# Attention, Fourier mixing and two MLPs on one core: the matmul that sums a pair's squares moves behind the step's score product in batches 2 and 3

## The chip, the cores and the metric

One core of a Trainium2 chip runs the whole program in one launch. The metric is device time in microseconds (us). The kernel before took 1077.4 us, the median of three runs (1074.99 to 1078.43).

## What is computed

Four batches of 8 heads, 576 tokens, head width 64. Cut to what matters:

```python
scores = q @ k.T / sqrt(64); bias = min(-(cum_i - cum_j), 0)   # cum = cumsum(relu(s))
attn = softmax(where(causal, -1e9, scores + bias)) @ v
x = attn.reshape(B, S, 512)
u = x + real(fft(fft(x, axis=1), axis=2))
x2 = u + relu(layernorm(u) @ w1) @ w2                # first MLP, 512 -> 2048 -> 512
out = x2 + relu((layernorm(x2) * g) @ w1b) @ w2b     # second MLP, same widths
```

## The kernel before, in words

**Order of the work.** The main stream is `MlpStream.run` (L582): the first MLP of a batch, chunk by chunk (L451 and L475 are its two products). Between two of its steps `side()` lets a generator emit work of the batches that come next: attention of batch b+1, then that batch's Fourier mixing (`fft_steps`), then its layer norm. So attention of batch 2 is woven into the MLP of batch 1, and attention of batch 3 into the MLP of batch 2; for batch 2 the first six pieces come earlier still, beside the mixing of batch 1. The second MLP runs last, alone (L517, L545).

The order in which each engine finally gets its instructions is not the order of the source text. A scheduler (L1572) places them on a modelled timeline by priority; an earlier place in the program is a higher priority, `urgent` (L1312) raises it for attention by a given number of places, and `tc.issue_after(x)` adds that an instruction on the engine of `x` must stand behind `x` there. Each engine works its queue off in that order.

**Attention in batches 2 and 3.** `attn_steps` (L933) goes over the batch's 4 pairs of heads. A pair has ten units (five tiles of queries, A0, A1, M, B0, B1, by two heads), one per step `j` = 0 to 9. In a step, `emit_qk` (L811) writes each unit's scores: per tile and head two fp16 products (L821, L822) into one PSUM tile, in two halves for B0. DVE then adds the bias and takes the minimum (L823), ACT makes two exponentials (L856, L857), POOL or DVE the low half (L867), SP a transposing DMA (L871, L879), and seven steps later `emit_pv` (L883) multiplies by v (L899). In these batches A0 has two units in steps 0 and 1, and B0 follows in steps 2 and 3 (in pairs 8 and 12, the first of their batches, A1).

**Preparation of the next pair.** The steps also prepare pair p (8 to 11 in batch 2, 12 to 15 in batch 3) while pair p-1 is worked on; pair 8 alone is prepared ahead of its batch. `prep_pair` (L722) is a generator, advanced once a step from `j` = 1 on:

- `j` = 1: three ACT squares of q, k and v with a sum along the free axis (L728) into `mx`, then `total(mx)` (L88): one fp32 matmul of `mx` with a matrix of ones (L92) that sums over the partitions. The trace has two records for each such matmul.
- `j` = 2: `pow2_scale` (L101 to L106 on DVE) and two products of scales (L735, L738).
- `j` = 3: high and low half of q (L746 on ACT, L747 on DVE).
- `j` = 4: the same of k (L753, L757), then one transposing DMA of q and k (L762) on SP.
- `j` = 5: v (L1069, L1070).

`load_pair` (L696, loads L691 to L709 on SP) fills `raw` for the pair after. When pair p begins, `turn_pair` (L773 on DVE) reverses a part of what the transposing DMA wrote, and the first score reads it.

`total` and the scores take their PSUM tiles from the same pool, `ps_s`, of three (L43); the tile of `total` is free again when L101 has read it. In batches 0 and 1 another path (`prep_pair32`, `emit_qk32`) does the same with fp32 products and sums the squares of v alone.

```python
        mxa = total(mx)
        yield
        sc = scs[:, p % 8, :]
        pow2_scale(sc[:, 0:3], sc[:, 3:6], mxa, 15)
```

Of the kernel before, what the change touches and what calls it, by code (L numbers as in the profile page):

```python
# [33 lines left out]
def fused_kernel(ctx: ExitStack, tc, q, k, v, s, wa1, wa2, g_ln, wb1, wb2, tok_c, feat_c, ident_c, rev_c, bias_c, out):  # L34
    nc = tc.nc
# [19 lines left out]
    def ftile(name, t, h):  # L55
        return ring.tile([128, FW[t]], F32, tag=f"f{t}{h}", name=name)
# [31 lines left out]
    def total(parts):  # L88

        n = parts.shape[1]  # L90
        ps = ps_s.tile([128, 512], F32, tag="s", name="total")[:, 0:n]
        nc.tensor.matmul(out=ps, lhsT=ones.to_broadcast([128, 128]), rhs=parts, start=True, stop=True)  # L92
        return ps

    def pow2_scale(dst, inv, squares, limit):

        top = int((127 + limit + 63.5 - 0.05) * 2 ** 23)
        d = dst.bitcast(I32)  # L100
        nc.vector.tensor_scalar(  # L101
            out=d, in0=squares.bitcast(I32), scalar1=-0.5, scalar2=float(top), op0=ALU.mult, op1=ALU.add
        )
        nc.vector.tensor_scalar(out=d, in0=d, scalar1=float(167 << 23), scalar2=float(67 << 23), op0=ALU.min, op1=ALU.max)
        nc.vector.tensor_scalar(out=d, in0=d, scalar1=0x7F800000, scalar2=None, op0=ALU.bitwise_and)
        nc.vector.tensor_scalar(  # L106
            out=inv.bitcast(I32), in0=d, scalar1=-1.0, scalar2=float(254 << 23), op0=ALU.mult, op1=ALU.add
        )
# [609 lines left out]
    def scale_cum(p, h):  # L718
        P = pairs[p]
        nc.scalar.activation(out=P.cumb[h], in_=P.cumb[h], func=AF.Copy, scale=P.sc[:, 6:7])  # L720

    def prep_pair(p):  # L722

        P = pairs[p]
        b, hp = divmod(p, NPAIR)
        mx = small.tile([128, 3], F32, tag="mx", name="mx")
        for i in range(3):
            nc.scalar.activation(  # L728
                out=qk16[:, i].rearrange("p t n -> p (t n)").bitcast(BF16), in_=raw[:, i].rearrange("p t h d -> p (t h d)"), func=AF.Square, accum_out=mx[:, i:i + 1]
            )  # L730
        mxa = total(mx)
        yield
        sc = scs[:, p % 8, :]
        pow2_scale(sc[:, 0:3], sc[:, 3:6], mxa, 15)
        nc.vector.tensor_scalar(  # L735
            out=sc[:, 6:7], in0=sc[:, 0:1], scalar1=sc[:, 1:2], scalar2=8.0, op0=ALU.mult, op1=ALU.mult
        )
        nc.vector.tensor_scalar(  # L738
            out=sc[:, 7:8], in0=sc[:, 3:4], scalar1=sc[:, 4:5], scalar2=-0.125, op0=ALU.mult, op1=ALU.mult
        )  # L740
        P.sc = sc
        yield

        for h in range(2):
            hi = qk16[:, h, :, 64 * h:64 * h + 64]
            nc.scalar.activation(out=hi, in_=raw[:, 0, :, h, :], func=AF.Copy, scale=sc[:, 0:1])  # L746
            nc.vector.scalar_tensor_tensor(  # L747
                out=qk16[:, h, :, 64 - 64 * h:128 - 64 * h], in0=raw[:, 0, :, h, :], scalar=sc[:, 0:1], in1=hi,
                op0=ALU.mult, op1=ALU.subtract,
            )  # L750
        yield
        for h in range(2):
            nc.scalar.activation(  # L753
                out=qk16[:, 2 + h].rearrange("p t (r d) -> p t r d", r=2),
                in_=raw[:, 1, :, h:h + 1, :].to_broadcast([128, 5, 2, D]), func=AF.Copy, scale=sc[:, 1:2],
            )
            nc.vector.scalar_tensor_tensor(  # L757
                out=qk16[:, 4 + h, :, 64 * h:64 * h + 64], in0=raw[:, 1, :, h, :], scalar=sc[:, 1:2],
                in1=qk16[:, 2 + h, :, 0:64], op0=ALU.mult, op1=ALU.subtract,
            )  # L760
        P.qkT = qkTs[p % 2]
        nc.sync.dma_start_transpose(  # L762
            out=P.qkT.rearrange("p b (t n) -> p (b t) n", n=128), in_=qk16.rearrange("p b t n -> p (b t n)")
        )
        yield
        P.v = v_tile()
        split_v(P, raw[:, 2].rearrange("p t h d -> p t (h d)"))
# [7 lines left out]
    def q_rows(P, t, h):  # L775
        if t in (B0, B1):
            return P.qx[:, h, QX[t]]
        return P.qkT[:, h, QCOLS[t]]
# [32 lines left out]
    def emit_qk(us):  # L811

        P, t = pairs[us[0].p], us[0].t
        n = EXT[t]
        cuts = ((0, 288), (288, 576)) if n > 512 else ((0, n),)
        mns = [small.tile([128, 2], F32, tag="mn", name="mn", bufs=4) for _ in us]
        kT, qTs = P.qkT, [q_rows(P, t, u.h) for u in us]
        for i, (a, z) in enumerate(cuts):
            for u, mn, qT in zip(us, mns, qTs):
                ps = ps_s.tile([128, 512], F32, tag="s", name="s")[:, 0:z - a]  # L820
                nc.tensor.matmul(out=ps, lhsT=qT, rhs=kT[:, 2 + u.h, a:z], start=True, stop=False)  # L821
                nc.tensor.matmul(out=ps, lhsT=qT, rhs=kT[:, 4 + u.h, a:z], start=False, stop=True)  # L822
                gate[0] = nc.vector.tensor_tensor_reduce(  # L823
                    out=u.f[:, a:z], in0=ps, in1=u.f[:, a:z], scale=P.sc[:, 7:8],
                    scalar=mn[:, i - 1:i] if i else 3.0e38, op0=ALU.add, op1=ALU.min, accum_out=mn[:, i:i + 1],
                )
        for u, mn in zip(us, mns):
            emit_exp(u, mn[:, len(cuts) - 1:len(cuts)])
# [10 lines left out]
    def emit_exp(u, mn):  # L839
        P, t, h = pairs[u.p], u.t, u.h  # L840
        n = EXT[t]
        if h == 0 and u.k % 2 == 0:
            sums[0] = small.tile([128, 4], F32, tag="rs", name="rs", bufs=4)
        u.both = sums[0]
        u.rs = sums[0][:, 2 * (u.k % 2):2 * (u.k % 2) + 2]
        w = NKB[t] * 128
        if t in (B0, B1):
            u.w = htile("p16", t, h, 0)
            if w > n:
                nc.gpsimd.memset(u.w[:, 0:2 * w].rearrange("p (r w) -> p r w", r=2)[:, :, n:w], 0.0)  # L850
        elif h == 0:
            P.w[t] = htile2("p16", t, 0)
            u.w = P.w[t][:, 0:2 * w]
        else:
            u.w = P.w[t][:, 2 * w:4 * w]
        nc.scalar.activation(out=u.w[:, 0:n], in_=u.f[:, 0:n], func=AF.Exp, bias=mn, scale=-1.0)  # L856
        nc.scalar.activation(  # L857
            out=u.f[:, 0:n], in_=u.f[:, 0:n], func=AF.Exp, bias=mn, scale=-1.0, accum_out=u.rs[:, h:h + 1]
        )
# [205 lines left out]
    def v_tile():  # L1065
        return att.tile([128, 5, 2, 128], F16, tag="v16", name="v16", bufs=2)

    def split_v(P, rv):
        nc.scalar.activation(out=P.v[:, :, 0, :], in_=rv, func=AF.Copy, scale=P.sc[:, 2:3])  # L1069
        nc.vector.scalar_tensor_tensor(  # L1070
            out=P.v[:, :, 1, :], in0=rv, scalar=P.sc[:, 2:3], in1=P.v[:, :, 0, :], op0=ALU.mult, op1=ALU.subtract
        )

    def emit_qk32(u):
        P, t, h = pairs[u.p], u.t, u.h
        n = EXT[t]
        pe = u.p < NPAIR
        block = {A0: 1, A1: 129, M: 0, B1: 320, B0: 448}[t]
        if pe:
            u.f = ftile("sc", t, h)  # L1080
            g = 2 * u.p + h
        cuts = ((0, 288), (288, 576)) if n > 512 else ((0, n),)
        mn = small.tile([128, 2], F32, tag="mn", name="mn", bufs=4)
        for i, (a, z) in enumerate(cuts):
            ps = ps_s.tile([128, 512], F32, tag="s", name="s")[:, 0:z - a]
            if pe:
                nc.tensor.matmul(
                    out=ps, lhsT=PB["sel"][:, g:g + 1].to_broadcast([96, 128]), rhs=PB["k"][:, a:z], start=True, stop=False
                )
            masked = pe and a <= block < z  # L1090
            nc.tensor.matmul(  # L1091
                out=ps, lhsT=P.qT[:, QCOLS[t]], rhs=P.kT[h][:, a:z], start=not pe, stop=not masked,
            )
            if masked:
                nc.tensor.matmul(out=ps[:, block - a:], lhsT=PB["eye"], rhs=PB[t], start=False, stop=True)
            gate[0] = nc.vector.tensor_tensor_reduce(  # L1096
                out=u.f[:, a:z], in0=ps, in1=PB["zero"].to_broadcast([128, z - a]) if pe else u.f[:, a:z], scale=-1.0,
                scalar=mn[:, i - 1:i] if i else 3.0e38, op0=ALU.add, op1=ALU.min, accum_out=mn[:, i:i + 1],
            )
        emit_exp(u, mn[:, len(cuts) - 1:len(cuts)])  # L1100
# [475 lines left out]
```

## Time and profile before

| | us |
|---|---|
| median of three runs | 1077.4 |
| the profiled execution | 1072.82 |
| its span, first to last instruction | 1071.0 |
| PE busy in it | 964.8 (90%) |
| DVE busy | 670.8 (63%) |
| ACT busy | 588.3 (55%) |
| POOL busy | 458.7 (43%) |
| mean granted TensorE clock, share of full speed | 0.968 |

PE is TensorE's matmul, PEld its weight load, DVE VectorE, ACT ScalarE, POOL GpSimd, SPq the queue on SyncE that issues DMAs. A row of a timeline gives start in us, length in us, engine, line, operation, output and inputs by the program's names, and in brackets how long the engine was idle just before and what ended that. Several like instructions in a row are merged (x18). The sums of q, k and v are 3 columns wide (128x3), which tells the eight matmuls at issue from the others on L92.

### The profile page before, as it was taken

How to read it: one execution, taken by the hardware profiler on the slowest of the kernel's cores; microseconds unless marked ns; L12 is line 12 of the kernel's file. 1: busy time of each engine (PE TensorE's matmuls, PEld its weight loads, DVE VectorE, ACT ScalarE, POOL GpSimd, SP SyncE). 2: the span in 40 equal slices, each digit the busy share in tenths (PEclk: the TensorE clock that was granted, in tenths of full speed). 3: DMA queues.
4: the chain of work that ended last, by engine and by line, in shares of the span. 5: the costliest groups of instructions: out<-in, count | busy, mean ns of one | idle time of the engine just before them, and what ended most of it. 6: DMA issues, size and time to landing. Idle time of an engine off the chain costs nothing.

```text
span 1071.0 us, 22888 instructions
## 1 busy us (share of the span) xinstructions
PE 964.8 (90%) x8665; PEld 738.3 (69%) x8665; DVE 670.8 (63%) x1659; ACT 588.3 (55%) x1263; POOL 458.7 (43%) x766
## 2 busy tenths in 40 slices
PE   4676659998989899979989989899999999999998
PEld 3444337666666576657766656678888888888887
DVE  5989889657794464956559969754543543542342
ACT  5788659775695653777533466444444434343341
POOL 3535344544373551545610042454543544543452
PEclk9889878999999999999999999999999999999999
DMA  6999966986599980699934852021121111111000
GB/s 199 273 183 276 228 171 128 165 154 115 126 164 192 186 155 1 125 203 168 206 96 136 287 177 60 21 59 21 41 51 31 40 39 43 40 40 21 21 21 21
DMA packets 289063, 125.47 MB, mean 117 GB/s; under 512 B 272696, under 2 KB 272952, under 8 KB 286904
## 3 DMA queue, kind: packets, MB, share of 16 engines
q1 hardware_dynamic: 288312, 121.90, 51.4%
q0 software_dynamic: 640, 2.10, 0.7%
q8 instruction: 68, 1.11, 0.4%
q14 instruction: 43, 0.35, 0.1%
HBM read 61.50 MB, written 9.51 MB: 66 GB/s over the span
## 4 chain that ended last, share of the span: by engine, by line
PE 52%; DVE 20%; DMA 9%; issue 8%; ACT 5%; POOL 3%; SPq 3%; DVEq 0%; POOLq 0%; ACTq 0%
PE acc L545 15%; PE g1x L517 9%; PE g L517 9%; PE g L451 7%; PE g L475 6%; PE pv L899 2%; POOL p L867 2%; DMA pT<-p 2%; PE s L1091 2%; DMA wastage<-in_moe_w_ch_dram 2%; DMA first<-first 1%; DVE h L458 1%; DVE wblow L192 1%; DVE sc L823 1%; DMA unT<-u 1%
## 5 line engine op out<-in xcount | busy, mean ns | idle before, releaser
L451 PE MATMUL g<-unT,warows 128*128 128x256 f16 (+1 forms) x1920 | 220.4, 265 | 4.5 <-DMA unT<-u 3.8
L451 PEld LDWEIGHTS <-warows 128*128 128x128 f16 x1920 | 174.9, 99 | 44.8 <-issue 7.9
L475 PE MATMUL g<-wastage,h 128*128 128x512 f16 x756 | 184.4, 384 | 7.2 <-DVE h L458 5.1
L517 PEld LDWEIGHTS <-wbrows 128*128 128x128 f16 x1728 | 169.1, 98 | 20.2
L867 POOL TENSOR_TENSOR p<-sc,p 128x448 f16<-128x448 f32 (+4 forms) x152 | 142.1, 946 | 93.4 <-ACT sc L857 73.4
L531 DVE TENSOR_TENSOR wastage<-wastage 128x896 f16<-128x896 f32 x72 | 78.5, 1090 | 160.2 <-ACT wastage L530 157.7
L545 PEld LDWEIGHTS <-wastage 128*128 128x128 f16 x1512 | 147.9, 98 | 17.1
L475 PEld LDWEIGHTS <-h 128*128 128x128 f16 x864 | 82.9, 99 | 93.8 <-DVE h L458 11.6
L530 ACT CAST wastage<-wastage 128x896 f16<-128x896 f32 x72 | 67.5, 938 | 120.6 <-POOL wastage L528 120.6
L856 ACT ACTIVATE p<-sc,mn 128x576 f16<-128x576 f32 (+4 forms) x160 | 89.6, 576 | 43.5 <-DVE mn L823 17.1
L527 POOL TENSOR_TENSOR wastage<-wastage 128x128 f32<-128x128 f32 x72 | 51.4, 714 | 133.5 <-ACT wastage L524 133.5
L899 PEld LDWEIGHTS <-pT 128*128 128x128 f16 x1632 | 63.0, 100 | 56.5 <-DMA pT<-p 42.5
L899 PE MATMUL pv<-v,pT 128*128 128x64 f16 x1632 | 68.9, 196 | 36.5 <-DMA pT<-p 28.0
L517 PE MATMUL g1x<-unT,wbrows 128*128 128x256 f16 x864 | 101.5, 273 | 0.0
L517 PE MATMUL g<-unT,wbrows 128*128 128x256 f16 x864 | 100.9, 273 | 0.0
L857 ACT ACTIVATE sc<-sc,mn 128x576 f32<-128x576 f32 (+4 forms) x160 | 91.7, 574 | 1.3
L545 PE MATMUL acc<-wbbig,wastage 128*128 128x256 f16 x756 | 89.9, 273 | 0.0
L545 PE MATMUL acc<-wblow,wastage 128*128 128x256 f16 x756 | 87.9, 273 | 0.0
L804 POOL TENSOR_SCALAR_AFFINE_SELECT sc<-cumb 128x129 f32<-128x129 f32 (+4 forms) x120 | 61.8, 527 | 47.7 <-ACT cumb L720 26.0
L1091 PE MATMUL s<-first 128*128 128x288 f32 (+4 forms) x192 | 72.6, 476 | 3.6 <-DVE mn L1096 2.1
L458 DVE SCALAR_TENSOR_TENSOR h<-g,h 128x512 f16<-128x512 f32 (+1 forms) x80 | 50.4, 629 | 28.1 <-ACT h L457 27.8
L850 POOL MEMSET p<- 128x128 f16 x64 | 13.5, 212 | 114.9 <-DMA pT<-p 76.6
(239 smaller groups left out, 1553.0 us busy)
## 6 DMA issues: line engine op xcount, KB each, us to landing
wbbig<-in_moe_w_ch_dram SPq DMA_DIRECT2D x8, 1024.0 KB
wbbig<-in_moe_w_ch_dram SPq DMA_DIRECT2D x16, 512.0 KB
cumb<-cumd SPq DMA_DIRECT2D x24, 288.0 KB
wastage<-in_moe_w_ch_dram SPq DMA_DIRECT2D x6, 1024.0 KB
xset<-in_moe_w_ch_dram SPq DMA_DIRECT2D x9, 512.0 KB
x2d<-o SPq DMA_DIRECT2D x18, 256.0 KB
first<-in_q_dram SPq DMA_DIRECT2D x64, 64.0 KB
first<-in_k_dram SPq DMA_DIRECT2D x32, 128.0 KB
```

Of the source, the lines that this page charges most:

```text
L451: nc.tensor.matmul(out=ps[:, c * i:c * i + c], lhsT=ch.w.w1(lw, kk, m + i), rhs=ch.unT[:, 4 * lx + kk, 0:c], start=(n == 0), stop=(n == 23),)
L475: nc.tensor.matmul(out=ch.ps[j], lhsT=h[:, lh, c:c + 128], rhs=ch.w.w2(lw, m + i), start=(m + i + n == 0), stop=(m + i == MB - 1 and n == 2),)
L517: nc.tensor.matmul(out=ps, lhsT=ch.w.w1(lw, kk, m + 8 * half), rhs=ch.unT[:, 4 * lx + kk, :], start=(n == 0), stop=(n == 11),)
L530: nc.scalar.copy(out=h[:, 0], in_=r[:, 0:7])
L531: nc.vector.tensor_tensor(out=h[:, 1], in0=r[:, 0:7], in1=h[:, 0], op=ALU.subtract)
L545: nc.tensor.matmul(out=acc[key], lhsT=h[:, lh, ia], rhs=b[:, ib, lw], start=(m == 0 and i == 0 and not second), stop=(m == 7 and i == 2 an ...
L804: nc.gpsimd.affine_select(out=u.f[:, 0:n], in_=P.cumb[u.h][:, 0:n], pattern=[[-1, n]], compare_op=ALU.is_ge, fill=MASKED, base=base, chann ...
L856: nc.scalar.activation(out=u.w[:, 0:n], in_=u.f[:, 0:n], func=AF.Exp, bias=mn, scale=-1.0)
L857: nc.scalar.activation(out=u.f[:, 0:n], in_=u.f[:, 0:n], func=AF.Exp, bias=mn, scale=-1.0, accum_out=u.rs[:, h:h + 1])
L867: eng.tensor_tensor(out=u.w[:, w:w + n], in0=u.f[:, 0:n], in1=u.w[:, 0:n], op=ALU.subtract)
L899: nc.tensor.matmul(out=ps[:, c], lhsT=pT[:, lp * nb + kb, :], rhs=P.v[:, kb, lv, c], start=(n == 0), stop=(n == 3 * nb - 1),)
L1091: nc.tensor.matmul(out=ps, lhsT=P.qT[:, QCOLS[t]], rhs=P.kT[h][:, a:z], start=not pe, stop=not masked,)
```

## The change

`total(mx)` is emitted in the step after the squares, ahead of `pow2_scale`, and it must stand on PE behind the last score product emitted so far. `last_qk` holds that product; the two functions that emit scores set it.

```diff
+    last_qk = [None]
+
     def prep_pair(p):
...
-        mxa = total(mx)
         yield
+        with tc.issue_after(last_qk[0].ins):
+            mxa = total(mx)
         sc = scs[:, p % 8, :]
         pow2_scale(sc[:, 0:3], sc[:, 3:6], mxa, 15)
...
                 nc.tensor.matmul(out=ps, lhsT=qT, rhs=kT[:, 2 + u.h, a:z], start=True, stop=False)
-                nc.tensor.matmul(out=ps, lhsT=qT, rhs=kT[:, 4 + u.h, a:z], start=False, stop=True)
+                last_qk[0] = nc.tensor.matmul(out=ps, lhsT=qT, rhs=kT[:, 4 + u.h, a:z], start=False, stop=True)
...
             if pe:
-                nc.tensor.matmul(
+                last_qk[0] = nc.tensor.matmul(
                     out=ps, lhsT=PB["sel"][:, g:g + 1].to_broadcast([96, 128]), rhs=PB["k"][:, a:z], start=True, stop=False
                 )
             masked = pe and a <= block < z
-            nc.tensor.matmul(
+            last_qk[0] = nc.tensor.matmul(
                 out=ps, lhsT=P.qT[:, QCOLS[t]], rhs=P.kT[h][:, a:z], start=not pe, stop=not masked,
             )
```

## Rows read from the trace of the kernel before

**Rows 1.** Busy time by stretch: PE, PEld, DVE, ACT, POOL, clock, DMA share, GB/s

```profile
270.00:400.00 130.00, 117.58 (x1140) 83.78 (x1139) 84.60 (x270) 88.95 (x212) 65.38 (x116) 0.97 0.87 165
...
430.00:540.00 110.00, 101.76 (x1101) 71.80 (x1100) 77.28 (x260) 75.60 (x180) 57.30 (x92) 0.97 0.94 188
```

**Rows 2.** Who waited for whom, 250 to 520 us: sum, times, longest

```profile
DVE scs L101 <- PE total L92: 11.5, 5, 5.0
...
PE s L821 <- DMA first<-first: 5.9, 3, 4.4
...
PE total L92 <- ACT first L728: 5.3, 2, 4.0
```

**Rows 3.** The instructions of L92: count, ns min/median/max, first and last start

```profile
L92 PE MATMUL total<-mx,ones x32: 167/252/373, 16.0 to 492.2; 128*128 128x1 f32 x16, 128*128 128x3 f32 x16
```

**Rows 4.** Timeline around the sum for pair 12

```profile
362.40 1.01 PE L899 MATMUL pv<-v,pT 128*128 128x64 f16 x29
...
366.49 0.74 ACT L728 ACTIVATE first<-first 128x640 bf16<-128x640 f32 x1 [4.41 <-DMA first<-in_v_dram]
...
367.38 0.38 PE L92 MATMUL total<-mx,ones 128*128 128x3 f32 x2 [3.96 <-ACT first L728]
367.51 0.18 PEld L821 LDWEIGHTS <-first 128*128 128x128 f16 x1
...
367.68 0.26 PE L822 MATMUL s<-first 128*128 128x129 f16 x1
...
368.26 3.54 PE L451 MATMUL g<-unT,warows 128*128 128x256 f16 x18
```

**Rows 5.** Busy time and granted clock by microsecond after that wait

```profile
367.00:368.00 1.00, 0.62 (x6) 0.56 (x7) 0.16 (x1) 0.32 (x2) 0.00 (x0) 0.86 1.01 182
368.00:369.00 1.00, 1.00 (x6) 0.70 (x5) 0.92 (x5) 0.49 (x2) 0.20 (x1) 0.50 1.15 214
...
371.00:372.00 1.00, 1.00 (x11) 0.85 (x9) 0.00 (x0) 1.00 (x3) 0.00 (x0) 0.93 1.07 276
```

**Rows 6.** Timeline around the sum for pair 14

```profile
461.84 0.38 PE L92 MATMUL total<-mx,ones 128*128 128x3 f32 x2 [1.36 <-ACT first L728]
...
462.44 1.15 PE L451 MATMUL g<-unT,warows 128*128 128x256 f16 x9
...
464.85 0.29 PE L822 MATMUL s<-first,qx 128*128 128x288 f16 x1
```

**Rows 7.** Timeline around the sum for pair 10

```profile
303.43 0.35 PE L92 MATMUL total<-mx,ones 128*128 128x3 f32 x2 [0.42 <-DVE f L432]
...
303.95 0.29 DVE L773 COPY qx<-first 128x512 f16<-128x512 f16 x1
...
307.51 0.18 DVE L105 TENSOR_SCALAR scs<-scs 128x3 int32<-128x3 int32 x1
...
307.58 0.22 PE L822 MATMUL s<-first 128*128 128x129 f16 x1
...
308.59 0.56 ACT L746 ACTIVATE first<-first,scs 128x320 f16<-128x320 f32 x1
```

**Rows 8.** Timeline around the sum for pair 9

```profile
277.50 0.22 PE L822 MATMUL s<-first 128*128 128x129 f16 x1
```

**Rows 9.** Timeline from pair 14's halves to its first score

```profile
467.55 0.55 DVE L757 SCALAR_TENSOR_TENSOR first<-first,scs 128x320 f16<-128x320 f32 x1
...
468.70 0.53 SPq L691 DMA_DIRECT2D first<-in_q_dram  x1
...
471.55 4.54 SPq L762 DMA_TRANSPOSE first<-first  x1
...
479.31 0.29 PE L821 MATMUL s<-first 128*128 128x129 f16 x1 [4.37 <-DMA first<-first]
```

**Rows 10.** Timeline at another wait of PE, pair 11

```profile
333.33 0.64 PE L899 MATMUL pv<-v,pT 128*128 128x64 f16 x12 [2.64 <-DMA pT<-p]
```

**Rows 11.** Busy time and granted clock just after that wait

```profile
335.00:336.00 1.00, 1.00 (x7) 0.68 (x5) 0.00 (x0) 0.00 (x0) 0.00 (x0) 0.50 0.80 180
```

## The prediction made before the run

> **What bounds the kernel.** I read the busy times by stretch first. The change acts only in attention of batches 2 and 3, and there PE is the fullest engine: 117.6 of 130 us in one stretch and 101.8 of 110 in the other, while DVE and ACT lie at 65 to 70% [rows 1]. The granted clock averages 0.97 in both. So 12.4 + 8.2 = 20.6 us of idle PE is all that any reordering there can give back, beside what a lowered clock costs. I then asked the list of waits who makes PE idle. Two entries touch the change: PE waited 5.3 us in two places for ACT's square ahead of the sum, and 5.9 us in three places for the transposed q and k at a pair's first score [rows 2]. The first is what the change can cut; the second is what it can lengthen, since the sum stands in that chain. Last I read the timeline at each of the eight sums (16 records of 3 columns, two for each matmul [rows 3]). Six cause PE no wait by ACT; the sums for pairs 12 and 14 do.
>
> **The wait at pair 12.** PE ends its products with v at 363.4 and stands until 367.38, 3.96 us, because the square of v on ACT starts only at 366.49, when the load of v has landed [rows 4]. Behind the sum stand the score of unit A0, second head (done by 367.94), then the first half of B0, then 18 matmuls of the MLP. None of them needs the sum; they stand behind it because the queue is worked off in order. [...] At pair 14 the wait is 1.36 us [rows 6].
>
> **The change, part by part.** It adds and removes no instruction: of the eight matmuls, seven move on PE from ahead of A0's second score to somewhere behind it; pair 8's, prepared before its batch begins, is bound only to the last score of batch 1, which is past by then. The squares stay on ACT, pow2_scale stays in its step on DVE. The moved call issues no DMA and nothing on POOL; in the program it passes the bias of that step (POOL), its two exponentials (ACT), its transposing DMA (SP) and its products with v (PE), and shares none of their queues but PE's. The sum's PSUM tile now comes after the score's instead of before it; both are held as long as before, so I cost that at nothing, covered by DVE reading them in the same order; without the cover a score waits for L101.
>
> *Saved.* The score's load and two products take from 367.51 to 367.94, 0.43 us, partly beside the sum [rows 4]; at 0.3 us clear in each of the two places, they now run inside the wait: 2 x 0.3 = 0.6 us. The bounds are 0 (the score is not ready sooner) and the whole of both waits with the clock, 3.96 + 1.36 + 1.7 = 7.0 us. I take 0.6, as only the score is sure to pass: the edge orders the sum against nothing else, and the step before has nothing of its own left that is ready at that point but some products with v.
>
> In the row, the load for that score starts at 367.51, behind the sum's wait and not in it [rows 4]. [...]
>
> *Added wait.* L101 waits for a sum that comes later. In most places the score follows the sum at once, so the delay is 0.3 us. Two are longer. For pair 9 the score ends at 277.7, and that pair begins only at 303.95 [rows 7, 8]: 26 us of cover. For pair 10 the score ends at 307.80, so the sum moves from 303.43 to about 307.9, 4.4 us later [rows 7]. That sounds costly. But L105, whose result lets ACT start the high half of q, ended at 307.69, and ACT came free for it only at 308.59. After the change: 307.9, plus 0.35 for the sum, plus three DVE operations at 0.18, gives 308.8, or 0.2 us late. DVE was full of other work in between, which is the cover; without it the cost would be the 4.4 us.
>
> *Next in that chain.* For pair 14, L757 ended at 468.10. SP issued the first load of the next q at 468.70 and the transposing DMA behind five loads at 471.55 [rows 9]. So a delay has between 0.6 us of cover (if it pushes the loads, which overwrite what L747 and L757 read) and 3.45 us (if it does not). A delay of 0.3 us fits under either end: nothing. The cost of the whole change is between 0 and the slower case below; I take 0.2 us, nearest to the rows for pair 10.
>
> **Sum.** 0.6 - 0.2 = 0.4 us off the profiled execution: 1072.8 becomes 1072.4. That execution lies 4.6 us below the median of the three runs and below their fastest, so I carry the difference over, not the level: 1077.4 - 0.4 = 1077.0 us. About 0.3% (3.2 us) is what a measurement can tell here, so this is no change. The scheduler also replans what comes after each moved sum; with nothing in the rows to price this, I let it widen the forecast by some 3 us to both sides, 1074.2 to 1080.
>
> **Rivals.**
>
> *Faster: the sum sinks further.* It is a step later in priority, so products of the MLP may be placed ahead of it. At pair 12, 18 such matmuls follow 0.6 us of scores; at full speed 18 take 18/9 x 1.15 = 2.3 us [rows 4, 6]. Ahead of the sum they leave 3.96 - 0.6 - 2.3 = 1.1 us of wait and spare the 1.7 us of clock; at pair 14 the 9 matmuls of 1.15 us and the scores fill the 1.36. Gain 2.9 + 1.7 + 1.3 = 5.9: 1071.5 us. For it: nothing of that work needs the sum, and the place in program order is later. Against it: attention's priority is raised, and in the rows the sum, A0 and B0 stand packed together with MLP work only behind them. Chance 0.27.
>
> *The clock alone.* Even 3.7 us of wait might leave the clock up: 1.7 us more, 1075.3. Against it: 2.64 us of waiting at pair 11 was followed by 0.50 [rows 10, 11]. [...] Chance 0.05; as a time it stays within 0.3%.
>
> *Slower: the sum holds up the transposing DMA.* If the sum sinks behind the next step's score too, it runs behind 465.14 instead of at 461.84 for pair 14 [rows 6], 3.3 us later. It decides from 0.6 us of delay on: beyond that, L757, the loads and L762 move with it, and PE's wait of 4.37 us ahead of pair 14's first score [rows 9] grows by up to 2.7 us. The same can befall pair 11, where PE waited too: the two waits beside pair 14's share 5.9 - 4.4 = 1.5 us [rows 2]. Price between 2.7 and 5.4, taken as 4: 1081.4 us. For it: this wait is the longest of its kind and the sum heads its chain. Against it: five loads stand between L757 and the DMA. Chance 0.20.
>
> *It does nothing.* If every sum was already behind its score, the queues would not change: 1077.4. The rows show the opposite order at pairs 12, 10 and, by the timeline, at most others. Chance 0.02.
>
> **How the numbers follow.** The forecast has 0.46, the faster rival 0.27, the clock 0.05, the slower 0.20, nothing 0.02. Replanning puts a little of the forecast beyond 0.3% on the fast side, since PE's idle time is what it can fill: faster 0.31, same 0.48, slower 0.21. The range reaches from the whole bound, 1077.4 - 7.0 = 1070.4, to the slower rival, 1081.4; the forecast's own range is 1074.2 to 1080.
>
> **What would show it.** Right: in the seven places the score of A0's second head stands ahead of the sum on PE; PE's wait on ACT's square is still there, 3 us or more at pair 12 and about 1 at pair 14, with the MLP behind it; L101's wait of 5.0 us shrinks little; L762 leaves at the same distance from its pair's first score. The faster rival shows as MLP matmuls between score and sum, no wait on L728, and a clock of 1.00 there. The slower shows as a longer wait of L821 for the transposed q and k. Wrong altogether would be a change of more than 3 us with the waits at the sums as they were: then order elsewhere, SP's queue above all, has changed.

## The result: slower, and where the lost time shows

The changed kernel took 1086.01 us, the median of 9 runs (1080.46 to 1088.1), beside 1076.6 us for the kernel before on the same chip (9 runs, 1074.63 to 1079.39). The ratio is 1.0075, 95% interval 1.0059 to 1.0090. That is slower by 0.75%, and above the forecast's range.

The profiled execution of the changed kernel took 1086.01 us, the level of its median; that of the kernel before, 1072.82, lay 3.8 us below the 1076.6. So of the 13.2 us between the two profiles, 3.8 us are a difference of executions, and 9.4 us are the change's.

| | before | after |
|---|---|---|
| span of the profiled execution, us | 1071.0 | 1084.2 |
| PE busy | 964.8 | 973.6 |
| mean granted clock | 0.968 | 0.957 |

The two clocks are those of single executions. The nine runs of the changed kernel average 0.962, and the 115 runs of the kernel before that were timed beside the experiments average 0.961, so a lower clock over the whole run is not shown.

Line numbers of the changed kernel are higher by 2 from L728 on and by 3 from L735 on: the squares are L730, the transposing DMA L765, the pair's turn L776, the scores L824 and L825, the output of the products with v L915.

First the waits that the change was about, from the list of who waited for whom between 250 and 520 us in the changed kernel (sum in us, times, longest):

```profile
PE g L451 <- DMA unT<-u: 4.9, 1, 4.9
DVE scs L101 <- PE total L92: 4.2, 2, 2.9
PE total L92 <- ACT first L730: 0.4, 1, 0.4
```

PE's wait for the squares ahead of the sums fell from 5.3 us to 0.4, and DVE's wait for the sums from 11.5 to 4.2 [rows 2]. PE's longest single wait is now 4.9 us, for the transposed input of an MLP chunk, where it was 0.8 us before. The kernel did what the faster rival said at the sums, and became slower. The timeline at pair 12's sum shows the first half of that, and that the gain didn't stay:

```profile
366.00 0.82 PE L902 MATMUL pv<-v,pT 128*128 128x64 f16 x12 [3.33 <-DMA pT<-p]
366.63 2.11 PE L451 MATMUL g<-unT,warows 128*128 128x256 f16 x9
...
371.81 1.04 PE L902 MATMUL pv<-v,pT 128*128 128x64 f16 x30
372.69 0.36 PE L92 MATMUL total<-mx,ones 128*128 128x3 f32 x2
372.91 0.28 PE L824 MATMUL s<-first,qx 128*128 128x288 f16 x1
```

MLP matmuls now run ahead of the sum and it waits for nothing. But 6.7 us earlier PE stands 3.33 us for a transposed block of attention weights, nearly as long as the 3.96 us for the square [rows 4]; and behind that wait the granted clock is low again (0.59 over 366 to 370 us).

Where PE lost time is seen in its busy time by stretch. The columns are those of [rows 1]; first the kernel before, then the changed one:

```profile
385.00:440.00 55.00, 54.05 (x479) 36.76 (x476) 33.83 (x89) 23.78 (x56) 17.20 (x30) 1.00 0.33 62
440.00:510.00 70.00, 62.85 (x599) 43.60 (x599) 48.35 (x170) 52.26 (x126) 37.99 (x66) 0.95 0.96 178
```

```profile
385.00:440.00 55.00, 52.21 (x457) 34.90 (x456) 27.07 (x66) 20.23 (x50) 17.61 (x31) 0.97 0.33 69
440.00:510.00 70.00, 58.62 (x557) 40.47 (x555) 47.64 (x178) 50.96 (x116) 33.39 (x58) 0.95 0.90 173
```

In these 125 us PE was busy 6.1 us less (1.8 + 4.2) and got 64 matmuls less done (22 + 42). From 240 to 385 us, where the sums and preparations of batch 2 move, PE's idle time fell from 15.4 to 13.6 us and what the lowered clock cost (one less the granted clock, summed over the stretch) rose from 3.4 to 5.1: 18.8 us before and 18.7 after. In the stretch from 385 to 510 us the same sum rose from 11.5 to 19.3, and from 510 to 620 us from 5.4 to 8.0. So most of the loss appears at the seam between batch 2's attention and batch 2's MLP, after the places where batch 2's sums moved. The new wait stands there. First the kernel before, then the changed one, at the first MLP product of batch 2:

```profile
442.28 2.78 PE L451 MATMUL g<-unT,warows 128*128 128x256 f16 x24 [0.82 <-DMA unT<-u]
```

```profile
446.66 0.28 PE L825 MATMUL s<-first,qx 128*128 128x288 f16 x1
451.80 1.46 PE L451 MATMUL g<-unT,warows 128*128 128x256 f16 x6 [4.86 <-DMA unT<-u]
```

The MLP of batch 1 had run out, and the layer norm of batch 2 was not ready. Followed back, the mixing of batch 2 began its products at 404.5 instead of 397.5, and the last output of batch 2's attention came at 410.5 instead of 403.4. What PE had done instead can be counted: by 385 us the changed kernel had started 915 products of the first MLP and 1104 with v, the kernel before 897 and 1122. Following the lateness back in turn, I came to pair 9, though not without a break: the next pair's turn, pair 10's, was 8.7 us late (330.74 instead of 322.07), but pair 11's only 1.1 us (355.20 instead of 354.10). PE's timeline at pair 9's sum, first before, then after:

```profile
275.91 0.36 PE L92 MATMUL total<-mx,ones 128*128 128x3 f32 x2
```

```profile
274.42 4.11 PE L1239 MATMUL z<-feat,yT 128*128 128x257 f16 x36
278.36 0.49 PE L451 MATMUL g<-unT,warows 128*128 128x256 f16 x3
280.54 0.53 PE L902 MATMUL pv<-v,pT 128*128 128x64 f16 x12 [1.68 <-DMA pT<-p]
280.90 1.48 PE L451 MATMUL g<-unT,warows 128*128 128x256 f16 x12
282.21 1.24 PE L475 MATMUL g<-wastage,h 128*128 128x512 f16 x5
283.29 0.28 PE L92 MATMUL total<-mx,ones 128*128 128x3 f32 x2
```

Before, this sum ran ahead of the last mixing products of batch 1; now all 36 of them and MLP work of two kinds stand in front of it. It needs none of that, and A0's score, behind which it was to stand, was done before 273. It sank 7.4 us by its later place in the program, which is a lower priority: e1 below, which has the later place without the order behind the score, runs this sum at 283.91. The scales that follow it on DVE, first before, then after:

```profile
276.31 0.16 DVE L101 TENSOR_SCALAR scs<-total 128x3 int32<-128x3 int32 x1 [1.16 <-PE total L92]
...
277.21 0.21 DVE L738 TENSOR_SCALAR scs<-scs 128x1 f32<-128x1 f32 x1
```

```profile
285.95 0.15 DVE L101 TENSOR_SCALAR scs<-total 128x3 int32<-128x3 int32 x1
286.02 0.69 DVE L394 BATCH_NORM_STATS2 st<-xset 128x6 f32<-128x512 f32 x1
...
289.14 0.15 DVE L105 TENSOR_SCALAR scs<-scs 128x3 int32<-128x3 int32 x1
...
292.15 0.20 DVE L741 TENSOR_SCALAR scs<-scs 128x1 f32<-128x1 f32 x1
```

The chain from L101 to the last scale took 0.9 us before and takes 6.2 us now: it has landed among the mixing's and layer norm's work on DVE. The lateness grows at every step: 7.4 us at the sum, 9.6 at L101, 14.9 at the last scale, and 18.0 at the transposing DMA. That DMA and what it releases, first before, then after (for the pair's turn before, see the 303.95 of [rows 7]):

```profile
283.55 4.56 SPq L762 DMA_TRANSPOSE first<-first  x1
...
290.33 0.74 ACT L728 ACTIVATE first<-first 128x640 bf16<-128x640 f32 x1 [0.71 <-DMA first<-in_q_dram]
```

```profile
301.58 4.59 SPq L765 DMA_TRANSPOSE first<-first  x1
...
308.04 0.83 DVE L776 COPY qx<-first 128x512 f16<-128x512 f16 x1 [0.65 <-DMA first<-first]
...
308.06 0.23 PE L824 MATMUL s<-first 128*128 128x129 f16 x1 [0.74 <-DMA first<-first]
...
308.56 0.72 ACT L730 ACTIVATE first<-first 128x640 bf16<-128x640 f32 x1
```

From issue to release this DMA takes 308.04 - 301.58 = 6.5 us. If it took as long before, it was through at about 283.55 + 6.5 = 290.0, and pair 9 began at 303.95 for other reasons: 13.9 us of slack. Now it releases pair 9's turn and first score itself, 4.1 us late. It has a second follower: the squares of pair 10, which overwrite what the DMA reads, start at 308.56 instead of 290.33.

### The profile page after: what moved, and what is told of

It reads as the page before. It is cut to its first block, busy times and chain, and to the rows that moved or that the text cites. A ratio compares the mean times of both kernels' runs of the same rounds, so it can differ in the third digit from the quotient of the medians.

```text
span 1084.2 us, 22881 instructions
## 1 busy us (share of the span) xinstructions
PE 973.6 (90%) x8665; PEld 742.8 (69%) x8665; DVE 676.2 (62%) x1659; ACT 588.2 (54%) x1263; POOL 454.5 (42%) x766
## 4 chain that ended last, share of the span: by engine, by line
PE 46%; DVE 12%; DMA 7%; issue 5%; POOL 4%; ACT 2%; SPq 2%; POOLq 0%; DVEq 0%; ACTq 0%
PE acc L545 14%; PE g1x L517 8%; PE g L517 8%; PE g L451 6%; PE g L475 5%; POOL p L870 2%; DMA wbbig<-in_moe_w_ch_dram 2%; DMA first<-first 1%; DMA pT<-p 1%; PE y L1202 1%; DMA cumb<-cumd 1%; PE z L1239 1%; PE pv L902 1%; DVE wblow L192 1%; DVE h L458 1%
## 5 line engine op out<-in xcount | busy, mean ns | idle before, releaser
L451 PE MATMUL g<-unT,warows 128*128 128x256 f16 (+1 forms) x1920 | 223.2, 268 | 5.2 <-DMA unT<-u 4.9
L870 POOL TENSOR_TENSOR p<-sc,p 128x448 f16<-128x448 f32 (+4 forms) x152 | 138.5, 921 | 91.7 <-ACT sc L860 75.2
L1094 PE MATMUL s<-first 128*128 128x288 f32 (+4 forms) x192 | 75.5, 492 | 3.7 <-DVE mn L1099 2.2
```

The source lines that it names most:

```text
L451: nc.tensor.matmul(out=ps[:, c * i:c * i + c], lhsT=ch.w.w1(lw, kk, m + i), rhs=ch.unT[:, 4 * lx + kk, 0:c], start=(n == 0), stop=(n == 23),)
L870: eng.tensor_tensor(out=u.w[:, w:w + n], in0=u.f[:, 0:n], in1=u.w[:, 0:n], op=ALU.subtract)
L1094: last_qk[0] = nc.tensor.matmul(out=ps, lhsT=P.qT[:, QCOLS[t]], rhs=P.kT[h][:, a:z], start=not pe, stop=not masked,)
```

## The experiments

Each was timed in 5 rounds against the kernel before on the same chip; 0.2% is about what such a comparison tells. The expectations speak of four theories:

- **A**: each late sum makes its pair's transposing DMA late, and each pair adds its part.
- **B**: the time moves because the scheduler replans everything behind a moved sum, in either direction, whatever is late.
- **C**: pair 9's preparation is late, wherever its sum stands; PE hides that with MLP matmuls and lacks them at the seam.
- **D**, formed after the first eight runs: what costs is pair 9's transposing DMA; by way of it batch 2's attention ends late, then its mixing, layer norm and first MLP product.

### Parts of the change: e1 to e4

e1 emits the sum a step later, without the order behind the score. e2, e3 and e4 apply the whole change to pairs 8 to 11, to pairs 12 to 15, and to pair 9 alone.

```diff
-        mxa = total(mx)
         yield
+        mxa = total(mx)
```

```diff
-        mxa = total(mx)
-        yield
+        mxa = None if p in (9,) else total(mx); yield
+        with tc.issue_after(last_qk[0].ins) if p in (9,) else ExitStack(): mxa = mxa if mxa is not None else total(mx)
```

> The sum is emitted a step later, but without the edge behind the score. If the edge costs the time (a score that now holds the sum up), this runs as the kernel before, within 0.3%. If the later place in the program costs it (lower priority, so the sum sinks among the MLP's matmuls), this runs as the changed kernel, 0.5 to 1.0% slower than before. I expect the second: nearly all sums stand at the same rows of PE's queue with and without the edge.

Measured: 1.0034 (1.0016 to 1.0053).

> Only the sums of pairs 8 to 11 are moved. Theory A (a late sum makes the pair's transposing DMA and its first score late, pair by pair): about half of the loss, 0.3 to 0.5% slower. Theory B (each moved sum lets the scheduler replan the queues behind it, with an effect of either sign that does not add up): any value between 0.5% faster and 1% slower, and the sum of this and of batch 3 alone differs from the whole by more than 0.4%.

Measured: 1.0062 (1.0040 to 1.0084).

> Only the sums of pairs 12 to 15 are moved, those with the two waits of PE on the square among them. Theory A: the other half of the loss, 0.3 to 0.5% slower. Theory B: any value, and not the remainder of batch 2 alone. If only the waits at the sums counted, 0.3 to 0.5% faster, since both (3.96 and 1.36 us) lie here.

Measured: 1.0013 (0.9992 to 1.0034).

> Only pair 9's sum is moved; it sinks furthest (from 275.9 to 283 us in the changed kernel, with its transposing DMA 18 us later), but its pair starts only at 304 us. Theory A: less than 0.3% slower, for the 18 us are mostly cover. Theory B: the queues behind it change up to the end of batch 3's attention, so any value up to 1% either way.

Measured: 1.0041 (1.0022 to 1.0060).

The step alone already loses, so the order behind the score isn't needed for a loss. But e1 lost less than was expected and less than half of what the change loses, and no run shows what makes the rest. Batch 2 carries most of the loss and batch 3, where the two waits were, nothing that can be told; a gain of 0.3 to 0.5% from the two waits alone did not come. The two halves add up to the whole (0.62 + 0.13 = 0.75%), which B did not expect. One pair of eight, pair 9, costs 0.41%. That speaks against A, and B has no reason to point at one pair.

### Is it pair 9's lateness? e5 to e8

e5 leaves every sum in place and makes pair 9's scales late, and with them its halves, its transposing DMA and its v:

```diff
-        mxa = total(mx)
-        yield
+        mxa = total(mx); yield
+        if p == 9: yield
         sc = scs[:, p % 8, :]
-        pow2_scale(sc[:, 0:3], sc[:, 3:6], mxa, 15)
+        with tc.issue_after(gate[0].ins) if p == 9 else ExitStack(): pow2_scale(sc[:, 0:3], sc[:, 3:6], mxa, 15)
```

> No sum moves. For pair 9 alone the scales (L101 to L738) come a step later and behind that step's L823 on DVE, which puts L738 at the same place of DVE's queue as in the run that moves pair 9's sum alone. Theory C (the loss comes from pair 9's preparation being late, wherever its sum stands; PE hides it in place with MLP matmuls and lacks them at the seam, 385 to 510 us): about the same loss as that run, +0.3 to +0.4%, the transposing DMA of pair 9 near 300 instead of 283.6, PE idle of batch 2's attention (240 to 385) as before and 4 to 6 us more in 385 to 510. Rival: it is the place of the sum's matmul on PE that costs, so with the sum where it was no loss, within 0.15%. Theory B (any new plan costs or gains at random): no number, anything in +-0.6%.

Measured: 1.0150 (1.0124 to 1.0176), the largest loss of all. Pair 9's sum ran at 275.3; its scales and its DMA:

```profile
288.23 0.15 DVE L101 TENSOR_SCALAR scs<-total 128x3 int32<-128x3 int32 x1
...
300.89 5.10 SPq L762 DMA_TRANSPOSE first<-first  x1
...
308.10 0.28 DVE L773 COPY qx<-first 128x512 f16<-128x512 f16 x1
```

The sum's place on PE is not what costs. The DMA leaves when it does in the changed kernel, and the loss is there, four times what C expected and twice the whole change's. From 440 to 510 us PE was busy 51.50 us at a clock of 0.85:

```profile
440.00:510.00 70.00, 51.50 (x460) 34.91 (x459) 46.36 (x165) 44.01 (x105) 34.14 (x57) 0.85 0.81 157
```

There PE stands for something else than in the changed kernel:

```profile
445.90 0.37 PE L821 MATMUL s<-first 128*128 128x257 f16 x1 [4.14 <-DVE scs L101]
...
457.26 0.40 PE L821 MATMUL s<-first,qx 128*128 128x288 f16 x1 [5.36 <-DVE mn L823]
457.46 0.44 PE L822 MATMUL s<-first,qx 128*128 128x288 f16 x1
457.85 3.60 PE L451 MATMUL g<-unT,warows 128*128 128x256 f16 x18
```

By the releasers in brackets these are scores of pair 12, of batch 3, that wait for a PSUM tile of `ps_s` until DVE has read it: L101 of pair 12 and the biases (L823) stood on DVE among the mixing and layer norm of batch 2. With a third such wait of 1.43 us they come to 10.9 us, and the MLP had nothing to put in their place: its products pause from 441.28 to 457.85.

e6 lets the score pass but keeps the sum in its step, directly behind it:

```diff
-        mxa = total(mx)
-        yield
+        mxa = P.mx = mx if p > 8 else total(mx); yield
+        mxa = P.mx
...
-                emit_qk(us[i:i + 1])
+                emit_qk(us[i:i + 1]); _ = p < 4 * NPAIR and j == KN['PJ'] and setattr(pairs[p], 'mx', total(pairs[p].mx))
```

> In pairs 9 to 15 the sum is emitted in the step of its squares, right behind that step's score, so it lets the score of A0's second head pass and does not lose a step of priority. By the prediction's own terms: 0.4 to 0.6 us off, the waits on ACT's square at pairs 12 and 14 still there but shorter (3.4 and 1 us). Theory C: pair 9's scales are not late (L762 of pair 9 before 290), so no loss: within 0.15% of the kernel before. Theory A (late sum, late transposing DMA, pair by pair): a small part of the loss, up to +0.2%. Theory B: no number, anything in +-0.6%.

Measured: 0.9983 (0.9967 to 0.9999). PE's wait on the squares is still there, 3.2 us in two places instead of 5.3:

```profile
PE total L92 <- ACT first L728: 3.2, 2, 2.7
```

e7 is the whole change with pair 9 left out (`p in (9,)` of e4 becomes the other seven pairs).

> The whole change with pair 9's sum left where it was. Theory C with pair 9 carrying most of the loss: 0.75 less 0.41, so +0.2 to +0.4%, pair 9's transposing DMA near 284, and less PE idle in 385 to 510 than the whole change's 11.4 + 2.8. Theory A with every pair adding its part: +0.6%. If pair 9 is the whole cause: within 0.15%.

Measured: 0.9972 (0.9953 to 0.9990), better than any theory had it: faster than the kernel before, and of all versions run the lowest median, 1073.92 us. Pair 9's DMA leaves on time:

```profile
283.49 4.57 SPq L762 DMA_TRANSPOSE first<-first  x1
```

e8 is the whole change with the preparation of a pair begun a step earlier (`'PJ': 0` for `'PJ': 1`).

> The whole change, and the preparation of pairs 9 to 15 begins at step 0 instead of step 1, so squares, sum, scales and halves all come a step earlier than in the changed kernel and the sum is emitted in the step where it stood before. Theory C: pair 9's chain is on time (its transposing DMA near 284), so most of the loss is back: between 0 and +0.3%. Theory A: the same. Rival (the edge behind the score itself costs): the loss stays, +0.6% or more. Theory B: no number.

Measured: 0.9978 (0.9961 to 0.9996), a little better than C expected; pair 9's DMA leaves at 283.5.

With the sums moved and pair 9's preparation on time (e7, e8) the change gains 0.2 to 0.3%; with the sums unmoved and that preparation late (e5) the kernel loses 1.5%. Pair 9's preparation decides. But e6 contradicts a part of C: there pair 9 begins at 307.5, nearly as late as in the changed kernel (308.0), and nothing is lost. Its start alone can't be the cause; in e6 the DMA had left at 284.4 and the squares of pair 10 began at 291.6.

### Which link of pair 9's preparation? e9 to e15

e9 and e13 leave sum, scales and halves alone and put only pair 9's transposing DMA later, e13 by two steps more. The edit is e13's; e9 is the same without the line `if p == 9: yield; yield`:

```diff
-        nc.sync.dma_start_transpose(
+        if p != 9: nc.sync.dma_start_transpose(
...
         split_v(P, raw[:, 2].rearrange("p t h d -> p t (h d)"))
+        if p == 9: yield; yield
+        with tc.issue_after(gate[1].ins): _ = p == 9 and nc.sync.dma_start_transpose(out=P.qkT.rearrange("p b (t n) -> p (b t) n", n=128), in_=qk16.rearrange("p b t n -> p (b t n)"))
```

> Sum, scales and halves of pair 9 stay where they are; only its transposing DMA (L762) is put a step later, behind the transposing DMA of the weights of that step (L871 or L879), so it should leave near 300 instead of 283.6. Theory D (what costs is that DMA: pair 9's start and the squares of pair 10, which overwrite what it reads, wait for it; with them batch 2's attention ends later, then its mixing and layer norm, and the first MLP product of batch 2, at 443.1 before and 451.8 after the change, stands waiting when the MLP of batch 1 has run out): pair 9 starts 3 to 5 us late, the last product with v of batch 2 later by 4 us or more, and +0.3% or more. Rival (it is DVE's and ACT's work on scales and halves in a worse place, the DMA has slack): within 0.2%. Theory B: no number, +-0.3%.

Measured: 0.9992 (0.9975 to 1.0008). The DMA left 10.9 us late, not at 300, and cost nothing (the first MLP product of batch 2, which the expectation puts at 443.1 before, starts at 442.28 in the row shown with the result):

```profile
294.46 4.95 SPq L768 DMA_TRANSPOSE first<-first  x1
...
303.06 0.74 ACT L728 ACTIVATE first<-first 128x640 bf16<-128x640 f32 x1 [2.92 <-issue]
...
306.17 0.29 DVE L774 COPY qx<-first 128x512 f16<-128x512 f16 x1
```

The turn has no releaser in brackets: DVE came to it without standing still. Of 13.9 us of slack 10.9 had been used up. The squares of pair 10 began 12.7 us late, and that cost nothing either. So the run missed the point that it was to test, and e13 went further.

> As the run with pair 9's transposing DMA late, two steps later again, so that it should leave at 300 or later (there it left at 294.5 and cost nothing). Sum, scales, halves and the loads of pair 10 stay where they are. Theory D with the DMA as carrier: pair 9 starts at 307 or later, batch 2's attention ends at 407.5 or later (403.4 before, at most 406.6 in every run without a loss), PE stands 8 us or more ahead of the first MLP product of batch 2, and +0.4% or more. Theory D with another carrier (the late scales and halves on DVE and ACT, which also hold back the loads of pair 10): within 0.2%, no such stand.

Measured: 1.0053 (1.0034 to 1.0071).

```profile
302.46 4.72 SPq L769 DMA_TRANSPOSE first<-first  x1
...
309.18 1.13 DVE L775 COPY qx<-first 128x512 f16<-128x512 f16 x1 [1.00 <-DMA first<-first]
309.26 0.74 ACT L728 ACTIVATE first<-first 128x640 bf16<-128x640 f32 x1 [1.15 <-DMA first<-first]
```

Now the DMA itself releases the turn and the squares of pair 10, and the loss is there with everything ahead of it on time. Beyond its slack, this one DMA suffices. Which of the two it releases carries the loss, the turn or the squares, no run separates. What was expected of the stand ahead of batch 2's MLP was wrong in size: 1.42 us instead of 8 or more.

```profile
448.16 1.03 PE L451 MATMUL g<-unT,warows 128*128 128x256 f16 x8 [1.42 <-DMA unT<-u]
```

PE was busy less on both sides of that stand instead: 51.21 us from 385 to 440 us (54.05 before) and 102.40 us from 510 to 620 us (104.60 before).

e10 and e11 are e5 with the extra step taken out, and with three of them. In e11 pair 9's halves come behind pair 10's loads in the program, so they are made of pair 10's data: it computes something else, and only its times are used.

> As the run with pair 9's scales late, but without the extra step: L101 of pair 9 stands only behind the L823 last emitted, which puts L738 4 places later on DVE's queue instead of 36. Theory D: the transposing DMA of pair 9 within some 3 us of its old time (283.6), far inside its slack to pair 9's start at 304, so no change: within 0.3%, the first MLP product of batch 2 within 3 us of 443. Theory B (any new plan costs at random): +-0.6%, whatever that landmark does.

Measured: 1.0017 (1.0000 to 1.0035); the DMA left at 286.5.

> The same edge with three extra steps: L738 of pair 9 56 places later on DVE's queue, against 36 in the run that cost 1.5%. Theory D: the transposing DMA of pair 9 later than 305, pair 9's start at 311 or later, the first MLP product of batch 2 at 455 or later, and +1.2% or more. Theory B: no number; a loss under 0.6% would speak for it and against D.

Measured: 1.0069 (1.0044 to 1.0093); the DMA left at 307.7, pair 9 began at 314.2. A loss, but little more than half of what D expected, and half of that of e5, whose DMA left 7 us earlier: the lateness doesn't set the size.

e12 is e4 for pair 10.

> The change for pair 10's sum alone: the queues differ for some 400 matmuls of PE and are the same again from there on. The prediction's own term for it was 0.2 us lost (the sum some 4 us later, covered on DVE). Theory D: no change, within 0.2%, the first MLP product of batch 2 within 1.5 us of 443. Theory A (every late sum costs its part): +0.1 to +0.3%.

Measured: 0.9999 (0.9980 to 1.0017), as expected. This is the place for which the prediction had worked out 0.2 us. But the chain behind the sum is later than that. Pair 10's sum ran at 308.90, its L105 ended at 312.30, and the high half of q, released by it, started 3.7 us after the 308.59 of [rows 7]:

```profile
312.33 0.56 ACT L746 ACTIVATE first<-first,scs 128x320 f16<-128x320 f32 x1 [1.11 <-DVE scs L105]
```

The transposing DMA of pair 10 left at 319.60 instead of 315.68, and pair 10's turn, which it releases, came 4.1 us late (326.12). None of it cost time.

e14 holds back the mixing of batch 2; e15 puts pair 10's loads two steps later:

```diff
                     pre = KN["KPRE"][b]
+                    for _ in range(4 * (b == 1)): yield
```

```diff
-                    if j == KN["PL"] and p + 1 < 4 * NPAIR:
+                    if j == (8 if p == 9 else KN["PL"]) and p + 1 < 4 * NPAIR:
```

> No pair is touched: in the kernel before, the generator that emits batch 2's Fourier mixing gives up four of its turns first, so mixing and layer norm of batch 2 come later among the MLP's steps. Theory D (attention of batch 2, mixing, layer norm, first MLP product of batch 2 is the chain that sets the end): that product starts x us later than 443 to 448, where runs without a loss have it, and the time grows by about x; with x of 5 us or more, +0.3% or more. Rival (the seam has slack; pair 9's lateness costs through the pairs of batch 3): the product later, the time within 0.2%. If the product does not move, the run tells nothing.

Measured: 0.9987 (0.9967 to 1.0007). The first MLP product of batch 2 stayed where runs without a loss have it, so the run tells nothing of the seam.

> The loads of pair 10 are emitted two steps later (step 8 instead of 6), all else as before. In the runs that lose, the squares of pair 10 start at 305 instead of 290. If late loads of pair 10 carry the loss: squares at 300 or later and +0.3% or more. If not, or if the loads are issued no later for it: within 0.2%.

Measured: 1.0007 (0.9987 to 1.0026). The squares started at 293.3, hardly later than the 290.3 of before: it tells little. e9, whose squares began at 303.06 without a loss, tells more.

### All of them side by side

From each trace (us): when pair 9's transposing DMA was issued, when pair 9's turn began, and the last output of batch 2's attention.

| kernel | ratio to before | DMA of pair 9 | turn of pair 9 | attention of batch 2 ends |
|---|---|---|---|---|
| e7, all but pair 9 | 0.9972 | 283.5 | 304.4 | 402.9 |
| e8, a step earlier | 0.9978 | 283.5 | 304.7 | 406.6 |
| e6, same step | 0.9983 | 284.4 | 307.5 | 403.5 |
| e14, mixing held back | 0.9987 | 283.9 | 304.4 | 404.7 |
| e9, DMA late | 0.9992 | 294.5 | 306.2 | 406.0 |
| e12, pair 10 | 0.9999 | 285.0 | 305.4 | 405.4 |
| before | 1 | 283.6 | 304.0 | 403.4 |
| e15, loads late | 1.0007 | 283.0 | 304.4 | 404.6 |
| e3, batch 3 | 1.0013 | 284.3 | 304.7 | 405.1 |
| e10, little late | 1.0017 | 286.5 | 304.0 | 406.2 |
| e1, step alone | 1.0034 | 302.5 | 309.0 | 410.8 |
| e4, pair 9 | 1.0041 | 300.4 | 306.9 | 407.6 |
| e13, DMA later | 1.0053 | 302.5 | 309.2 | 409.0 |
| e2, batch 2 | 1.0062 | 300.5 | 307.0 | 410.6 |
| e11, scales later | 1.0069 | 307.7 | 314.2 | 413.1 |
| the change | 1.0075 | 301.6 | 308.0 | 410.5 |
| e5, scales late | 1.0150 | 300.9 | 308.1 | 415.8 |

Seven kernels issue that DMA at 300.4 or later, and all seven lose 0.34% or more. Nine others issue it at 294.5 or earlier, and none of them is more than 0.17% slower than the kernel before. The end of batch 2's attention divides them in the same way, at 407.6 against 406.6. So do the products of the first MLP started by 385 us, 911 or more against 903 or fewer, and the squares of pair 10, 307.0 or later against 303.1 or earlier. The queues were replanned differently in each, and yet the DMA tells who loses: that answers B as far as the sign goes. Within the group that loses, none of the three columns orders the ratios.

The pause of the MLP at the seam comes nearer to the size. The longest stretch without an MLP product on PE that begins between 436 and 460 us is 1.7 to 5.1 us in the ten kernels that do not lose. In those that lose, in the order of the table, it is 8.0, 8.4, 2.6, 8.5, 11.1, 8.6 and 16.6 us. e5 has the longest. e13, with 2.6, loses in another way, on both sides of the seam.

**Shown**: without pair 9's late sum the change loses nothing (e7), and pair 9's transposing DMA alone brings a loss when it is late beyond its slack (e13) and none within it (e9). **Read in the traces, not isolated**: that in the change it is this DMA, and nothing else of pair 9's late preparation; and the road from there, by the end of batch 2's attention, the mixing and the layer norm, to PE standing at the seam. **Open**: what sets the size at the same lateness, from 0.34% in e1 to 1.5% in e5, where the waits for PSUM tiles at pair 12 are the difference that the trace shows; and how much of the 0.75% is pair 9's own: moved alone its sum costs 0.41%, moved beside the other seven about 1.0% (0.9972 to 1.0075), so these parts do not add up.

## Why the prediction was wrong, step by step

**The step that failed** is in "Added wait": "For pair 9 the score ends at 277.7, and that pair begins only at 303.95: 26 us of cover." Three things were wrong in it.

- The sum didn't come right behind the score. It sank to 283.29, behind mixing and MLP products. The text priced a later place as if only the score could come between, and allowed sinking only in rivals, at pairs 11, 12 and 14.
- The delay was taken as constant along the chain. It grew from 7.4 to 18.0 us, since each link had to find its place anew on a queue full of other work. At pair 10 I had looked at the links on DVE and ACT, and taken DVE's other work for cover; at pair 9, with 26 us of cover, I had not looked at them.
- The cover was measured from the wrong end. What has to be ready at 303.95 is the transposed data, and the DMA took 6.5 us from issue to release in the changed kernel (301.58 to 308.04) and 6.7 in e13 (302.46 to 309.18). With 6.5 us its slack to the turn was 13.9 us, an estimate, not 26, and the squares of pair 10 wait for it too.

**Saved.** 0.6 us was taken, with the whole of both waits, 7.0 us with the clock, as the far end. Of these the clock's 1.7 us are an estimate from the trace of before: after the wait at pair 12 the granted clock was 0.86, then 0.50 in three whole microseconds, then 0.93 (367 to 372 us, in part [rows 5]), so 0.14 + 3 x 0.50 + 0.07. For the waits themselves the far end was nearer: 5.3 us became 0.4. But the whole did not gain by it: shortly ahead of pair 12's sum PE now stands 3.33 us for a transposing DMA, with the granted clock at 0.59 from 366 to 370 us, which is 4 x 0.41 = 1.6 us of full speed lost. With the score let past and the sum kept in its step, the thing I had priced, e6 gained 0.17%, 1.8 us of 1077; the 0.6 us lies inside its interval (0.1 to 3.6 us).

**Pair 10 and pair 14.** Priced at 0.2 us and at nothing. e12 measured nothing for pair 10 alone, and e3 nothing that can be told for batch 3. For pair 10 that was luck: its half came 3.7 us late where 0.2 had been worked out, because DVE's other work, named as the cover, now stood between the links. The price came out because pair 10's turn, 4.1 us late, cost nothing.

**The PSUM tile.** Costed at nothing, with the case that a score waits for L101 as the exception. In the changed kernel no score waited for L101 from 250 to 520 us. PE's waits ahead of scores for DVE's reading of an earlier score did rise, from 2.8 us in three places to 5.5 in seven; no run shows how much of that is the sum's.

**Replanning**, some 3 us to both sides. Among the kernels whose pair 9 was on time the ratios run from 0.9972 to 1.0017, that is -3.0 to +1.8 us. The allowance held for what it meant, and pair 9's chain is not in it.

**The rivals.** The faster one described the sums as they came out, and its gain of 5.9 us didn't come: removing a wait of PE is a gain only if nothing else is late then. With pair 9 left out, e7 gains 0.28%, 3.0 us of it. The slower one had the mechanism, "the sum holds up the transposing DMA", but the wrong pair, and its sign did not show: PE's waits for the transposed q and k came to 5.8 us in four places, against 5.9 in three. I put it where a wait already showed (pairs 14 and 11) and took 0.6 us as the point from which it decides. Where it struck, no wait showed before, because 13.9 us of slack hid it; it decided between 10.9 us of delay (e9) and 16.9 us (e4, whose DMA left at 300.4). Its price, 4 us, was less than half of the 9.4 us measured, so the range ended 4.6 us too low.

## What to carry to other kernels

A later place in the program is a lower priority: ask of a moved instruction not what it must stand behind, but what may now be put in front of it, link by link down to the transfer at its chain's end. Measure the cover at that transfer, with its duration, and not at the instruction that moved; a link with no wait in the profile may be hidden by a slack that the change uses up. When a stage absorbs a delay by doing other work early, look for the price where that work was meant to fill a gap: here over 100 us later, and the cure was to leave one pair of eight as it was.

## Unexpected

By the faster rival the clock was to gain where PE's waits went. No gain shows: the nine runs of the changed kernel average 0.962, and those of the kernel before 0.961 (0.954 to 0.969 singly). What differs between the two profiles is where the clock is low. Behind the wait at 451.80, from 452 to 456 us, it averaged 0.68, where at the same product before, after a stand of 0.82 us, it stayed at 1.00 (442 to 446 us). In the changed kernel it was 0.50 from 448 us on, within the stand, and at 1.00 again from 455 us. So the stand of 4.9 us at the seam went with 1.3 us of lowered clock beside its length (4 x 0.32). The kernel before has its low stretch later, 0.50 from 477 to 483 us, around PE's wait of 4.37 us at pair 14 [rows 9]; over the whole 440 to 510 us both average 0.95. The row of the changed kernel, with the columns of [rows 1]:

```profile
452.00:456.00 4.00, 4.00 (x27) 3.12 (x26) 4.00 (x17) 1.27 (x5) 3.94 (x7) 0.68 0.98 195
```
